# A new hand-written order of the engines' work in a fused HGRN2 and PReLU-network kernel

## The chip, the cores and the metric

The kernel runs on one core of one Trainium2 chip. The metric is the device time of one execution in microseconds (us). The kernel before took 596.71 us as the median of three runs (596.15, 596.71 and 600.7).

## The reference

Two blocks follow each other. The first is a gated linear attention (HGRN2) on q, k, v and f_logit of shape (4 batches, 8 heads, 768 tokens, 48); its output, bridged to 3072 tokens of 384, goes through a two-layer network with a PReLU.

```python
def _attn_ref(q, k, v, f_logit):
    f = 1.0 / (1.0 + np.exp(-f_logit))
    state = np.zeros((B, H, D, D), dtype=np.float32)
    for t in range(S):
        state = f[:, :, t, :, None] * state + np.einsum('bhd,bhe->bhde', k[:, :, t], v[:, :, t])
        y[:, :, t] = np.einsum('bhd,bhde->bhe', q[:, :, t], state)

def _moe_ref(x, w_in, w_out, alpha):      # w_in 384 x 2048, w_out 2048 x 384
    h = x @ w_in
    g = np.maximum(h, 0.0) + alpha * np.minimum(h, 0.0)
    return g @ w_out
```

## The kernel before, in words

The work is cut into 12 steps. Step n takes batches 2·(n % 2) and the one after it, and chunk n // 2 of 128 tokens (`steps`, L937). A step has an attention part, which gives xT (384 x 256 tokens), and a network part on that xT. The attention of step n+1 is laid between the network of step n, so that TensorE (PE) always has work.

Each step's work is split into some sixty closures, and `ORDER_WORDS` (L41 to L88) is a list of words, one for each closure; the loop at L957 calls them in that order. The scheduler is set to manual for PE, VectorE and ScalarE, so each engine's queue holds its instructions in just this order; the DMA issues of SP and POOL follow the same list. A word is the step's number and a key: `5r0` is the raw scores of step 5's first batch, `4Na3` the fourth slice of step 4's network. The keys that matter here:

- Loads. `e`: f, q, k and v of the step (L305 to L323), on POOL's queue except in step 0. Each load waits until the last reader of the tile before it is done.
- Gates and scans. `f` (ScalarE: the sigmoid at L329, then copies), `F` (VectorE lags at L338), `g` (ScalarE copies of the scores, L365), `G`, `h`, `i`, `k`, `l`, `p`, `q`, `t`: chiefly VectorE scans and products, some ScalarE copies.
- Scores. `r0`, `r1`: raw scores on PE (`scored`, L576; 64 loads and matmuls each); `R0`, `R1`: their copying to ad on VectorE (L599). `u0`, `u1`: scores by quads on PE (`scored4`, L585); `U0`, `U1`: their copying (L451). `o`: off-diagonal scores on PE (L566), `O`: copies on ScalarE (L573). `A0`, `A1`: placing in A on ScalarE (L606).
- State and output. `K`: the keys turned by way of DRAM, four DMA writes (`turned`, L473) and one read (`ksn`, L475), both on SP's queue. `d`: the state's increments on PE (L539); `D`, `M`: the state on VectorE (L544). `y0`, `y1`: the output products on PE (L614); `Y0`, `Y1`: their copies on ScalarE (L494). `X`: y to DRAM and back as xT (L503 to L505).
- Network, first layer. `Nx`, `Ny`, `Nz`: xh, xl and xs made from xT on ScalarE; `NY`, `NZ`: adding DMAs on POOL's queue (xl<-xT, xs<-xl, L823). `Na0` to `Na7`: the eight slices of x·w_in on PE (L831). From step 3, slices 3 to 6 go by parts: two passes in `Na`, a scaling on ScalarE in `Nq`, and a third pass with xs in `Nb`. `Nr` (ScalarE, L854) and `Nc` (VectorE, L859) apply the PReLU.
- Network, second layer. From step 1 its product is done in seven block products `Np0` to `Np6` (banks pa, pc, pb, pa, pd, pe, pf; L886), whose operands are sums of the gate made by `Nm`, `Nu`, `Nv`, `Nw` on VectorE (L880). `Nk`, `Ng` (ScalarE, L917 and L921) and `Nd`, `Ne`, `Nf`, `Nh`, `Ni`, `Nj`, `Nl`, `NL` (VectorE, L896) put the output together; `Ns0`, `Ns1` store it on SP's queue.

PSUM is held by two pools. `psa` has two pairs of banks, for raw, qu, off, pd, py and pk of the attention; `psn` has four banks for the network. A product that needs a bank waits until the bank's last reader is done.

```python
    with tc.manual_schedule(engines={mybir.EngineType.PE, mybir.EngineType.DVE, mybir.EngineType.Activation}):
...
        for key in ORDER:
            run[key]()
```

Of the kernel before, what the change touches and what calls it, by code (L numbers as in the profile page):

```python
# [40 lines left out]
ORDER_WORDS = """  # L41
0e 1e 0I0 0f 0F 0G 0g 0h 0i 0m 0p 0j 0r0 a0 0r1 0I1 0l 0I2 0R0 0I3 0I4 0I5 a1 0q 0o 0O 0k a2 0s 0t 0K0 w0 0u0 0U0
0R1 0J0 0H0 1f 0J1 0J2 0u1 0U1 0K1 0A0 1F w1 0d 0D 0J3 0H1 0J4 0A1 0J5 w2 0y0 0J6 0Y0 b0 0y1 0M 1G 0x0 0Y1 1r0 1g
1R0 0x1 0X a3 1h a4 0J7 1i w3 1r1 a5 2e 0Na0 0Nr0 0Na2 1R1 b1 w4 0Na1 0Na3 a6 1j 0Nc0 w5 0Nr1 v0 0Na4 0Na5 0Nc1 1m
0Nr2 1l 1k 0Nr3 a7 0Nc2 0Nr4 1o b2 v1 1K0 w6 b3 w7 0Nc3 0Na6 1K1 1p 0Nc4 1O 0Na7 v2 b4 1q 0Nr5 0Nc5 1u0 0Nr6 b5 0Nc6
0Nr7 v3 2f 1U0 0Nc7 b6 1u1 1U1 0Np0 1H0 1A0 2F 1H1 v4 1s 0Np1 0Np2 v5 1d b7 v6 V 1t v7 0Np3 0Np4 1D 1A1 1y0 1y1 2g
1Y0 0Np5 W0 1Y1 1X W1 W2 0Np6 W3 2G 1Na0 W4 W5 0Np7 0No0 1M 2h 0No1 2i Y3 1Na3 1Nr0 1Na1 Y4 Y5 2p 1Nr1 2q W6 Y6 1Na2
1Na4 1Nr2 2r0 2u0 2l W7 1Nc0 1Na5 1Nr3 1Nc1 2k 1Nm0 1Nr4 2K 1Nc2 2t 1Nc3 1Nm1 1Nc4 1Na6 1Nr5 2R0 1Nr6 2r1 2U0 2u1
1Nc6 2R1 1Na7 2A0 3e 1Nr7 1Nc5 2o 2U1 1Np0 Z3 2O 1Nc7 2d Z4 1Nk 1Np2 2D 2A1 3f 3F 1Np1 2y0 2y1 2Y0 1Np3 2Y1 2X 1Nu0
3g 1Nu1 1Nv0 3G 1Np4 1Nd 1Nv1 1Nw0 1Ng 1Nw1 1Ne 1Nj 1Nh 1Np5 3h 1Np6 1Nf 3p 1Nl 1Ni 3i 2Na2 2Na0 2M 1NL 2Na1 2Nr0 3l  # L50
3t 2Nr1 2Na3 3q 2Na4 2Nr2 3r0 3u0 2Nc0 2Nr3 3k 2Nc1 2Nm0 3K 2Nc2 3R0 3U0 2Nc3 2Na5 2Nm1 2Nr4 3r1 2Nr5 3o 3R1 2Na6
3A0 4e 2Nc5 3u1 2Nr6 2Nc4 3O 3U1 1Ns1 Z5 2Na7 2Nc6 Z6 3A1 3d 3D 1Ns0 2Np0 2Nr7 2Np1 2Nk 2Nc7 4f 2Nd 3y0 T 3y1 4F 3M
# [9 lines left out]
5Nz 5NZ 5Na5 6K 5Nc2 5Na4 6R0 5Nr7 5Na3 6U0 5Nc7 6r1 5Nq3 6A0 6u1 6R1 6U1 5Nq4 7e 5Nb3 5Nq5 4Ns0 5Na6 5Nb4 6o 5Nr3
5Nq6 5Nc3 6O 6A1 6d 5Nm1 5Nb6 5Nb5 6D 5Nr4 5Nr5 5Np0 5Nr6 5Nc4 5Nc6 7f 6y0 5Nc5 7F 6y1 5Nk 7g 6Y0 6Y1 5Np2 5Np1 6X
6M 5Np3 5Nu0 5Ng 5Nu1 5Nv0 5Nv1 5Nw1 7G 5Np4 6Nx 6Ny 5Nw0 5Nd 5Ne 7h 5Nj 5Nh 5Np5 5Np6 5Nf 7p 5Nl 5Ni 5Ns1 6Nz 6NY
6Na0 7i 7l 6Nr0 6Na1 5NL 6Na2 7k 7q 6Nr1 6Nc1 6Nr2 6Nc0 6Na7 6Na3 6Nm0 7r0 7K 6Nc2 7u0 7R0 6Nr7 6NZ 7t 7U0 7A0 6Na5
6Na4 6Nq4 7u1 6Nq3 6Nc7 7r1 6Nq5 6Na6 7R1 5Ns0 7U1 6Nq6 8e 6Nb3 6Nr3 6Nc3 6Nb4 6Nm1 6Nb6 6Nb5 7o 6Nr4 6Nr5 7A1 7O
# [5 lines left out]
9r0 9p 7Nl 7Ni 7Ns1 8Nz 8NY 8Na0 8Na7 9i 8Nr0 8Na1 7NL 8Na2 9k 8Na5 9l 9q 9u0 9t 8Nr1 8Nr2 8Nc0 8Na3 9R0 8Nc2 8Nc1
9K 8Nr7 8Na4 8NZ 8Nm0 9U0 8Nq4 9A0 8Nq3 8Nq5 9r1 9u1 8Na6 8Nc7 9R1 9U1 8Nq6 10e 8Nb3 8Nb4 8Nr3 8Nc3 8Nm1 8Nb6 8Nb5
8Nr5 9o 7Ns0 8Nr4 8Nc5 9A1 8Nr6 9O 9d 8Np0 8Nc4 9D 8Nk 8Np1 8Nc6 10f 9y0 9y1 8Np2 10F 9Y0 9Y1 10g 9X 9M 8Np3 8Nu0
8Nu1 10G 8Np4 9Nx 8Nd 10r0 8Nv0 8Nv1 8Nw0 8Ng 8Np5 8Ne 8Nw1 10h 9Ny 8Nh 8Nj 8Np6 8Nf 10p 8Nl 8Ni 9Nz 9NY 9Na0 9Nr0
8NL 10i 9Na1 9Na2 10k 10l 9Na7 10q 10t 9Nr1 9Nr2 9Nc0 9NZ 9Nc2 9Nc1 10K 9Nr7 10R0 8Ns1 9Na3 9Nm0 9Nc7 9Na4 10u0 10U0
9Na5 9Nq3 9Nq4 9Nb4 9Nq5 8Ns0 9Na6 10A0 9Nq6 11e 9Nb3 10r1 9Nr3 10u1 9Nb5 9Nc3 10R1 9Nb6 9Nm1 9Nr4 9Nr5 9Np0 10U1
9Nr6 9Nc6 10o 9Nc5 10d 10A1 10O 9Nc4 10D 11f 9Nk 9Np1 9Np2 10y0 10M 11F 9Nd 11G 10y1 10Y0 10Y1 9Np3 9Ng 11g 10X 9Nu1
9Nu0 9Nv0 9Np4 9Nv1 9Nw0 9Np5 9Ne 9Nw1 10Nx 9Nj 9Nh 11h 9Np6 9Nf 11p 9Nl 9Ni 10Ny 9NL 10Nz 10NY 10Na0 11i 9Ns1 10Nr0
10Na1 10Na2 10NZ 11k 11l 11q 10Na7 11r0 11t 10Nr1 10Nr2 10Nc0 10Nc2 11u0 10Nc1 10Nr7 10Nm0 11R0 11K 10Na3 11U0 10Nq3  # L80
10Na4 10Nq4 11A0 9Ns0 10Na6 10Nq6 10Nc7 10Na5 10Nb3 10Nb4 11u1 10Nr3 11r1 10Nr4 10Nc3 10Nq5 10Nm1 10Nb6 11R1 10Nb5
10Nr5 10Np0 11d 11U1 10Nr6 10Nc5 11o 10Nc6 11A1 10Nc4 11O 11D 10Nk 10Np1 10Np2 10Nd 10Nu0 11y0 10Nu1 11y1 11Y0 10Nv0
10Nv1 11Y1 11M 11X 10Np3 10Nw0 10Ng 10Ne 10Nw1 10Np4 10Np5 10Nj 11Nx 10Nh 11Ny 11Na7 10Nf 10Nl 10Ni 11Nz 11NY 11Na0
10Np6 11Nr0 11Na1 10NL 11Na2 11Nc0 11Na3 10Ns1 11Nr1 11Nc1 11Nm0 11Nr2 11Na4 11NZ 11Nc2 11Nr7 11Na5 11Nq3 11Nq4
10Ns0 11Na6 11Nq5 11Nb3 11Nc7 11Nq6 11Nb4 11Nr3 11Nb5 11Nc3 11Nr4 11Nr5 11Nm1 11Nb6 11Np0 11Nc4 11Nr6 11Nc5 11Nc6
11Nk 11Np1 11Np2 11Nd 11Np3 11Nu0 11Nu1 11Nv0 11Nv1 11Np4 11Nw0 11Ng 11Ne 11Nw1 11Np5 11Nj 11Nh 11Nl 11Np6 11Nf 11Ni
# [928 lines left out]
```

## Time and profile before

| | |
|---|---|
| median of three runs | 596.71 us (596.15 to 600.7) |
| profiled execution | 601.4 us, its span 599.6 us |
| PE busy, matmuls | 97% of the span, 8,200 |
| PEld busy (weight loads) | 89%, 8,200 |
| VectorE (DVE) busy | 84%, 1,027 instructions |
| ScalarE (ACT) busy | 50%, 561 instructions |
| GpSimd (POOL) busy | 11%, 114 instructions |
| mean granted TensorE clock | 0.982 |
| DMA | 67.57 MB, 113 GB/s in the mean |

All times within the profile count from the span's start. In a timeline row the first number is the start and the second the length in us; a number in brackets at the end is the idle time before the instruction and what released it ("issue": nothing that the profile shows), and x at the end a count of like instructions taken together. In the view of waits the three numbers are us in total, times, and the longest.

### The profile page before, as it was taken

How to read it: one execution, taken by the hardware profiler on the slowest of the kernel's cores; microseconds unless marked ns; L12 is line 12 of the kernel's file. 1: busy time of each engine (PE TensorE's matmuls, PEld its weight loads, DVE VectorE, ACT ScalarE, POOL GpSimd, SP SyncE). 2: the span in 40 equal slices, each digit the busy share in tenths (PEclk: the TensorE clock that was granted, in tenths of full speed). 3: DMA queues.
4: the chain of work that ended last, by engine and by line, in shares of the span. 5: the costliest groups of instructions: out<-in, count | busy, mean ns of one | idle time of the engine just before them, and what ended most of it. 6: DMA issues, size and time to landing. Idle time of an engine off the chain costs nothing.

```text
span 599.6 us, 18858 instructions
## 1 busy us (share of the span) xinstructions
PE 582.6 (97%) x8200; PEld 530.7 (89%) x8200; DVE 506.5 (84%) x1027; ACT 301.9 (50%) x561; POOL 68.5 (11%) x114
## 2 busy tenths in 40 slices
...
GB/s 300 348 159 375 62 54 28 178 54 54 177 56 93 190 56 79 184 52 91 173 72 67 137 109 80 151 107 80 140 119 80 125 133 52 109 47 29 80 1 26
DMA packets 69443, 67.57 MB, mean 113 GB/s; under 512 B 44689, under 2 KB 58641, under 8 KB 69361
## 3 DMA queue, kind: packets, MB, share of 16 engines
...
q8 instruction: 64, 1.05, 0.7%
...
q14 instruction: 19, 0.15, 0.1%
...
## 4 chain that ended last, share of the span: by engine, by line
PE 83%; DVE 8%; ACT 6%; issue 2%; DMA 1%; ACTq 0%; DVEq 0%
PE ph L831 39%; PE pa L886 7%; PE pe L886 5%; PE pf L886 5%; PE pd L886 4%; PE qu L591 4%; PE pc L886 3%; PE pb L886 3%; PE raw L582 3%; PE po L866 3%; PE py L614 3%; DVE qd L338 2%; ACT A L606 2%; PE pd L539 1%; DVE ad L451 1%
## 5 line engine op out<-in xcount | busy, mean ns | idle before, releaser
L831 PE MATMUL ph<-xT,w_in_sb 128*128 128x256 f32 x612 | 136.9, 380 | 0.4 <-DMA xT<-y 0.3
L831 PEld LDWEIGHTS ph<-xT,w_in_sb 128*128 128x128 f32 x612 | 115.1, 190 | 16.8 <-issue 0.9
L854 ACT ACTIVATE gate<-ph 128x512 f32<-128x512 f32 x96 | 55.0, 595 | 121.2 <-PE ph L831 107.6
L859 DVE SCALAR_TENSOR_TENSOR gate<-gate,om,ph 128x256 f32<-128x256 f32 x192 | 81.2, 475 | 31.3 <-ACT gate L854 31.0
L886 PE MATMUL pa<-w_out_sb,gate 128*128 128x192 f32 x352 | 61.7, 329 | 0.0
L880 DVE TENSOR_TENSOR gate<-gate 128x512 f32<-128x512 f32 x88 | 57.5, 687 | 3.6 <-PE pb L886 2.8
L886 PEld LDWEIGHTS pa<-w_out_sb,gate 128*128 128x128 f32 x352 | 57.1, 190 | 0.5
L451 DVE COPY_PREDICATED ad<-mquad,qu 128x224 f32<-128x224 int32 (+6 forms) x140 | 42.2, 301 | 6.8 <-PE qu L591 1.6
L599 DVE COPY_PREDICATED ad<-mraw,raw 128x256 f32<-128x256 int32 (+1 forms) x96 | 42.6, 444 | 5.9 <-PE raw L582 3.3
L606 ACT COPY A<-ad 32x256 f32<-32x256 f32 x96 | 38.7, 403 | 11.7 <-DVE ad L451 10.2
L844 ACT ACTIVATE ph<-ph 128x512 f32<-128x512 f32 x36 | 20.0, 570 | 37.6 <-PE ph L831 25.1
L440 DVE TENSOR_TENSOR scores<-scores,fs 128x768 f32<-128x768 f32 (+5 forms) x60 | 37.4, 623 | 1.6
L831 PE MATMUL ph<-xh,hi 128*128 128x256 f32 x216 | 35.3, 300 | 0.0
L831 PE MATMUL ph<-xl,lo 128*128 128x256 f32 x216 | 32.7, 289 | 2.2 <-issue 2.2
L424 ACT COPY A<-q 48x512 f32<-48x512 f32 x44 | 27.1, 617 | 15.2 <-DVE q L398 14.8
L886 PE MATMUL pb<-t,gate 128*128 128x192 f32 x176 | 31.5, 331 | 0.5 <-DVE gate L859 0.5
L886 PE MATMUL pd<-t,gate 128*128 128x192 f32 x176 | 30.6, 327 | 1.0 <-DVE gate L880 1.0
L831 PEld LDWEIGHTS ph<-xh,hi 128*128 128x128 f32 x216 | 29.4, 194 | 2.5 <-issue 1.2
L831 PEld LDWEIGHTS ph<-xl,lo 128*128 128x128 f32 x216 | 29.3, 197 | 2.4 <-issue 2.4
L338 DVE TENSOR_TENSOR qd<-qd,f 128x768 f32<-128x768 f32 (+2 forms) x36 | 27.2, 754 | 4.6 <-ACT qd L331 4.6
L886 PE MATMUL pe<-w_out_sb,gate 128*128 128x192 f32 x176 | 30.6, 327 | 0.4 <-DVE o L896 0.4
L323 POOL DMA_DIRECT2D vs<-in_v x22 | 13.2, 605 | 154.6 <-PE py L614 154.4
...
## 6 DMA issues: line engine op xcount, KB each, us to landing
...
```

Source lines behind the costliest of these rows:

```text
L338: nc.vector.tensor_tensor(qdv[d], qdv[d - 1][:, :, :, 1:5 - d], f[:, :, 1:5 - d].rearrange("p (g i) r -> p g i r", i=NB), ALU.mult)
L424: nc.scalar.copy(A[halves(cc)[1], :, par * HP:(par + 1) * HP, CH * cc:CH * (cc + 1)], x["q3"][rows(par)].rearrange("p (u h c) s t -> p u h ...
L440: nc.vector.tensor_tensor(by_four(us[:, :, UO[m]:UO[m] + 4 * n]), by_four(us[:, :, skip:skip + 4 * n]), spread(fq[:, :, 1:1 + n], n), ALU. ...
L451: nc.vector.copy_predicated(ad[:, u, :, :, 4 * m:DB], mquad[:, lo:lo + n].bitcast(I32).unsqueeze(1).unsqueeze(1).broadcast_to((128, 2, HP, ...
L591: nc.tensor.matmul(qu[DB * j:DB * (j + 1), par, hp * QS + 4:hp * QS + QL], lhsT=x["k4"][r_, g * DB:(g + 1) * DB], rhs=x["us"][r_, g, 4:QL] ...
L599: nc.vector.copy_predicated(adu[:, :, :, d:4], mraw[:, d, :, d:4].bitcast(I32).unsqueeze(1).broadcast_to((128, H, NB, n)), rv[:, :, QO[d]: ...
L606: nc.scalar.copy(A[s_, u, :, s_], ad[s_, u].rearrange("p r h t -> p (r h) t"))
L831: nc.tensor.matmul(banks[f][:, j * T:(j + 1) * T], lhsT=of[:, kt, 128 * j:128 * (j + 1)], rhs=by[:, kt], start=first_ and kt + j == 0, sto ...
L854: nc.scalar.activation(to, of, AF.Relu, scale=-1.0)
L859: nc.vector.scalar_tensor_tensor(to[:, j], to[:, j], om[:, m:m + 1], of[:, j], ALU.mult, ALU.add)
L880: nc.vector.tensor_tensor(block(to)[:, p], block(x_)[:, p], block(y_)[:, p], op)
L886: nc.tensor.matmul(banks[to][:, 0:DH], lhsT=block(of)[:, f], rhs=of_w_out(by)[:, f], start=start and f == 0, stop=f == NH - 1, skip_group_ ...
```

## The change: the same words in another order

Only `ORDER_WORDS` is changed. It holds the same words as before, each once; no closure, tile, pool or queue differs, and every engine gets the same number of instructions of each kind (PE 8,200 matmuls). On PE at least 36 of 331 words stand elsewhere, on VectorE 42 of 470, on ScalarE 33 of 312, on SP 13 of 61, on POOL 2 of 29.

The main moves:

- PE: `4r0` from behind the first products of network 3 to between `2Np3` and `2Np4`. `5r0` from beside `5u0` to ahead of `4Na0`, so that five slices of network 4 lie between the two. `8r0` and `8u0`, which stood together, have `7Na3` and `7Na7` between them, and `7Na4` goes behind `8u0`. `10r0` between `8Np3` and `8Np4`, `9r0` one word earlier. Two slices of network 2 between `3u0` and `3r1`, and `3o` behind `2Na7 2Na6`. In steps 6 and 7 almost nothing moves (`6Na4` and `6Na5` change places).
- ScalarE: xs earlier (`3Nz`, `4Nz`, `5Nz` ahead of `Nr0` of their step, where they stood behind it). `7g` behind `6Y0 6Y1`. `8f` ahead of `7O`. `9g` behind `8Y0 8Y1`.
- VectorE: `6M` behind `5Nd` and `7G` earlier; `8U0` ahead of `7Nc7`; `8q` behind `7Nc0`; `9R0` ahead of `9i`; `2M` ahead of `1Nw1`.
- SP: stores (`Ns0`, `Ns1`) behind the turned keys or the tokens of the next step. POOL: the loads of step 3 go q, f, k instead of q, k, f; network 5's xs<-xl goes ahead of the load of q for step 7, which it followed.

The stretch from `2Np2` on, which shows the moves of `4r0`, `3Nz` and the first part of step 4:

```diff
-3Y0 3Y1 2Np2 2Np3 2Nu1 2Nu0 4G 2Np4 3X 2Nv0 4g 2Nv1 2Nw0 2Ng 3Nx 3Ny 2Nw1 2Ne 2Nj 2Nh 2Np5 4h 2Np6 2Nf 4p 2Nl 2Ni
-3Na0 4i 3Nr0 2NL 3Na2 3NY 4k 4l 4q 2Ns1 3Nz 3Na1 4t 3Nr1 3Na7 3Na4 3Nr2 3Nc0 4K 3Nc2 3Nc1 4r0 3Nr7 3Nm0 4u0 3Nc7
-3Na6 3NZ 2Ns0 4R0 3Na3 4U0 4r1 3Na5 4u1 3Nq3 3Nq4 4A0 3Nq5 4R1 4U1 3Nq6 4o 4O 5e 3Nb3 3Nr3 3Nc3 3Nb4 3Nm1 3Nb6 3Nb5
+2Np2 1Ns0 3Y1 3M 4g 2Np3 4r0 2Nu1 2Nu0 2Np4 3X 2Nv0 4G 2Nv1 2Nw0 2Ng 3Nx 3Ny 2Nw1 2Ne 2Nj 2Nh 2Np5 4h 2Np6 2Nf 2Nl
+4p 3Na1 3Nz 3Na0 4i 3Nr0 2NL 2Ni 4k 4l 3NY 3Na2 4q 3Nr1 3Na7 4K 3Na3 5e 2Ns1 3Nr2 3Nc0 3NZ 3Na4 3Nc2 4t 3Nc1 3Nr7
+3Nm0 4u0 3Nc7 4R0 4U0 3Nq3 3Na6 4r1 4A0 4R1 3Na5 4u1 4U1 3Nq4 3Nq5 3Nq6 4o 4O 3Nb3 3Nr3 3Nc3 3Nb4 3Nm1 2Ns0 3Nb6
```

Step 5 between the products of network 4:

```diff
-3Nw0 3Ng 5G 3Np4 4Nx 4Ny 3Nw1 3Nd 3Ne 5h 3Nj 3Nh 3Np5 3Np6 3Nf 5p 3Nl 3Ni 4Na0 5i 4Nr0 3NL 4Na2 4NY 5k 4Na5 5l 3Ns1
-4Nz 4Nq5 4Na1 5q 5t 4Nr1 4Nc0 4Nr2 5r0 5u0 4Nc1 4Nm0 5K 4Nc2 5R0 4NZ 4Na3 5U0 4Na7 4Nr7 4Na4 5r1 5A0 4Nq3 4Nq4 5u1
-4Nc7 5R1 5U1 4Na6 4Nb4 6e 4Nb3 5o 4Nq6 4Nr3 5d 5O 4Nc3 5A1 4Nm1 5D 4Nb6 4Nb5 4Nr4 4Nr5 4Np0 4Nr6 5y0 3Ns0 4Nc4 4Nc5
+5G 3Nv1 3Nw0 3Ng 3Np4 4Nx 4Ny 3Nw1 3Nd 3Ne 5h 3Nj 3Np5 3Np6 3Nh 3Nf 3Nl 5p 3Ni 5r0 4Nz 4Na0 5i 4Nr0 4Na1 3NL 5k 4NY
+4Na5 5l 4Nq5 4Na2 5q 4Nr1 5K 4Na3 4Nc0 4Nr2 5u0 5t 4Nc1 4Nm0 4Nc2 5R0 5U0 4Na7 4Nr7 4NZ 4Na4 6e 3Ns1 5r1 4Nc7 4Nq4
+4Nq3 5A0 5u1 5R1 5U1 4Na6 4Nb5 4Nb3 5o 4Nq6 4Nr3 5d 5O 4Nc3 4Nb4 5A1 4Nm1 5D 4Nr4 4Nr5 4Nb6 4Np0 4Nr6 5y0 4Nc4 4Nc5
```

Step 7 and 8, at the words that moved:

```diff
-5Nr6 5Nc4 5Nc6 7f 6y0 5Nc5 7F 6y1 5Nk 7g 6Y0 6Y1 5Np2 5Np1 6X
+5Nr6 5Nc4 5Nc6 7f 6y0 5Nc5 5Nk 7F 6y1 6Y0 5Np2 6Y1 5Np1 6X 7g
...
-6Nc4 6Nr6 7d 6Np0 8f 6Nc5 7D 6Nk 6Np1 7y0 8F 7y1 6Nc6 7Y0 7Y1 7X 6Np2 8g 7Nx 7M 6Np3 6Nu0 6Nu1 8G 6Np4 6Nv0 6Nd 6Nv1
+6Nr6 7d 8f 6Np0 7O 6Nc5 7D 6Nk 6Np1 7y0 8F 7y1 6Nc6 7Y0 6Np2 7Y1 7X 8g 7Nx 7M 6Np3 6Nu0 6Nu1 6Np4 6Nv0 6Nd 6Nv1 6Nw0
...
-8t 8r0 7Nr2 7Nc0 7Nc1 8u0 8R0 7Nm0 7Na7 8K 7Nc2 7Nr7 7Na3 7Nc7 7NZ 7Na5 8U0 7Nq3 7Nq4 8r1 8u1 7Nq5 8A0 6Ns0 7Na6 8R1
+7Nr2 7Nc0 8q 7Nc1 8R0 9e 6Ns1 8K 7Na3 7Nm0 7Na7 8u0 7Nc2 7Nr7 7NZ 7Na4 8U0 7Na5 7Nq3 7Nq4 8r1 8u1 7Nq5 8A0 7Na6
```

More of the change, by code (lines that the diff above doesn't have):

```diff
@@ L41 @@
 ORDER_WORDS = """
[L42 to L51, printed above, removed]
@@ L52 @@
-3A0 4e 2Nc5 3u1 2Nr6 2Nc4 3O 3U1 1Ns1 Z5 2Na7 2Nc6 Z6 3A1 3d 3D 1Ns0 2Np0 2Nr7 2Np1 2Nk 2Nc7 4f 2Nd 3y0 T 3y1 4F 3M
-3Y0 3Y1 2Np2 2Np3 2Nu1 2Nu0 4G 2Np4 3X 2Nv0 4g 2Nv1 2Nw0 2Ng 3Nx 3Ny 2Nw1 2Ne 2Nj 2Nh 2Np5 4h 2Np6 2Nf 4p 2Nl 2Ni
-3Na0 4i 3Nr0 2NL 3Na2 3NY 4k 4l 4q 2Ns1 3Nz 3Na1 4t 3Nr1 3Na7 3Na4 3Nr2 3Nc0 4K 3Nc2 3Nc1 4r0 3Nr7 3Nm0 4u0 3Nc7
-3Na6 3NZ 2Ns0 4R0 3Na3 4U0 4r1 3Na5 4u1 3Nq3 3Nq4 4A0 3Nq5 4R1 4U1 3Nq6 4o 4O 5e 3Nb3 3Nr3 3Nc3 3Nb4 3Nm1 3Nb6 3Nb5
-4d 3Nr4 3Nr5 3Np0 4D 4A1 3Nr6 3Nc6 3Nc5 4y0 3Nc4 4y1 5f 4M 4Y0 4Y1 3Np2 3Np1 3Nk 5F 4X 3Np3 3Nu0 5g 3Nu1 3Nv0 3Nv1
@@ L62 @@
[L62 to L66, printed above, removed]
@@ L72 @@
[L72 to L76, printed above, removed]
@@ L77 @@
[L77 to L86, printed above, removed]
@@ L87 @@
-11NL 11Ns1 11Ns0
+0e 1e 0I0 0f 0F 0G 0g 0r1 0h 0i 0m 0p 0j 0r0 0I1 0l 0I2 a0 0R0 0I3 0I4 0I5 0q 0o a1 0k a2 0O 0s 0t w0 0u0 0U0 0R1
+0K0 0H0 1f 0J0 0J1 0J2 w1 0K1 0u1 0J3 0U1 1F 0A0 0d 0D 0H1 0A1 w2 1G 0J4 0J5 0y0 0Y0 b0 0J6 0y1 0x0 0Y1 0M 1g 1i 0J7
+1r0 0x1 1R0 0X a3 1h a4 b1 w3 a5 1m 1r1 w4 1j 0Na0 v0 0Nr0 0Na1 0Na2 1R1 0Na3 a6 0Nc0 w5 0Nr1 0Na4 0Na5 0Nc1 2e 0Nr2
+1l 1k 0Nr3 a7 0Nc2 1o b2 0Nr4 1K0 1p 1O v1 w6 w7 0Na7 1K1 0Nc3 0Nc4 b3 v2 b4 0Na6 1q 0Nr5 0Nc5 1u0 0Nr6 b5 0Nc6 0Nr7
+v3 1u1 1s 2f 1U0 0Nc7 b6 1U1 1H0 1A0 2F 1t 0Np0 v4 0Np1 0Np2 v5 1d b7 v6 V 1H1 1D v7 2g 0Np3 0Np4 1A1 1y0 1y1 1Y0
@@ new lines @@
+0Np5 W0 1Y1 1X W1 Y3 W2 0Np6 W3 2G 1Na0 W4 W5 0Np7 0No0 2h 1M 0No1 2i 1Nr0 1Na1 Y4 Y5 1Na3 2p 1Nr1 2q W6 1Na2 1Na4
+Y6 3e 1Nr2 2u0 2l 1Nc0 1Nr3 2t 1Nc1 2k 1Nm0 1Nr4 1Nc2 2r0 1Nc3 W7 1Nm1 1Na5 1Nc4 1Na6 1Nr5 2R0 1Nr6 2r1 2U0 2K Z3
+2u1 1Nc6 2R1 2A0 1Na7 1Nr7 1Nc5 2o 1Np0 2U1 2O 3f 1Nc7 2d Z4 1Nk 2D 2A1 1Np2 3F 1Np1 2y0 2y1 1Np3 2Y0 2Y1 2X 1Nu0
+1Nu1 1Nv0 3G 3g 1Np4 1Nd 1Nv1 1Nw0 1Ng 2M 1Nw1 1Ne 1Nj 1Nh 1Np5 3h 1Np6 1Nf 1Nl 3p 1Ni 3i 1NL 2Na0 3l 4e 2Nr0 2Na1
+2Nr1 2Na3 2Na2 1Ns1 3q 2Nr2 3r0 3u0 2Nc0 2Nr3 3k 3t 2Nc1 2Nm0 3R0 3U0 2Na5 2Nc2 2Nc3 2Nm1 2Na4 Z5 2Nr4 3r1 2Nr5 3K
```

34 lines of the change are left out of this document (29 added, 5 removed).

## The prediction, made before the change was run

> **What bounds the kernel now.** I read the page first: busy shares, the share of the chain, and the DMA queues.
>
> ```profile
> PE 582.6 (97%) x8200; PEld 530.7 (89%) x8200; DVE 506.5 (84%) x1027; ACT 301.9 (50%) x561; POOL 68.5 (11%) x114
> ...
> q8 instruction: 64, 1.05, 0.7%
> ...
> PE 83%; DVE 8%; ACT 6%; issue 2%; DMA 1%; ACTq 0%; DVEq 0%
> ```
>
> TensorE carries the chain and has no spare share; the change leaves all its matmuls in place. So a new order can only win back the microseconds in which PE stands. I therefore went to the view of waits for PE and PEld, which names what ended each stand:
>
> ```profile
> PE pd L886 <- DVE gate L880: 1.0, 2, 0.7
> PE pb L886 <- DVE gate L859: 0.5, 1, 0.5
> PE pe L886 <- DVE o L896: 0.4, 1, 0.4
> PE qu L591 <- DVE ad L451: 0.2, 1, 0.2
> ...
> PEld ph L831 <- issue: 5.2, 16, 2.4
> ...
> PEld qu L591 <- issue: 3.0, 5, 1.7
> ...
> PEld off L566 <- issue: 2.0, 5, 1.1
> ```
>
> Two kinds are seen: PE waits for VectorE (five stands, 2.1 us), and PE stands on "issue", in which no engine is late. The largest of the second kind, in the timeline of PEld (start, us, idle before):
>
> ```profile
> 204.60 0.73 PEld L582 LDWEIGHTS raw<-qd,k 48*32 48x32 f32 x64
> ...
> 206.15 0.79 PEld L831 LDWEIGHTS ph<-xl,lo 128*128 128x128 f32 x6
> 207.08 0.83 PEld L591 LDWEIGHTS qu<-scores,k 48*32 48x32 f32 x64
> ...
> 209.13 0.58 PEld L566 LDWEIGHTS off<-q,kh 48*32 48x32 f32 x57 [1.08 <-issue]
> 209.75 2.33 PEld L831 LDWEIGHTS ph<-xs,sum 128*128 128x128 f32 x19
> ```
> ```profile
> 253.68 0.36 PEld L591 LDWEIGHTS qu<-scores,k 48*32 48x32 f32 x28 [1.67 <-issue]
> 254.22 1.35 PEld L831 LDWEIGHTS ph<-xh,hi 128*128 128x128 f32 x6 [0.17 <-issue]
> 255.45 1.40 PEld L831 LDWEIGHTS ph<-xl,lo 128*128 128x128 f32 x6
> ```
> ```profile
> 349.35 1.02 PEld L831 LDWEIGHTS ph<-xl,lo 128*128 128x128 f32 x6 [2.40 <-issue]
> 350.25 2.89 PEld L831 LDWEIGHTS ph<-xs,sum 128*128 128x128 f32 x13
> ```
>
> They break off in the middle of a word (7 of 64 loads of 4o, 36 of 64 of 5u1, within 6Na6), so they are no wait of the program. What are they? The windows between them, with PE, PEld, DVE, ACT and POOL busy (count), granted clock, DMA share and GB/s:
>
> ```profile
> 208.80:253.50 44.70, 43.12 (x634) 40.53 (x633) 40.86 (x86) 22.41 (x42) 5.22 (x7) 1.00 0.43 105
> 253.50:349.20 95.70, 93.09 (x1394) 87.59 (x1394) 85.39 (x178) 46.21 (x87) 10.44 (x14) 0.98 0.44 108
> ```
> ```profile
> 251.40:254.30 2.90, 1.47 (x95) 1.06 (x79) 2.24 (x6) 2.39 (x6) 0.72 (x1) 0.98 0.85 223
> 346.10:349.40 3.30, 1.11 (x19) 0.82 (x7) 2.87 (x7) 2.05 (x5) 0.72 (x1) 1.00 0.88 295
> 240.00:260.00 20.00, 18.57 (x446) 16.77 (x448) 14.77 (x42) 8.80 (x18) 2.20 (x3) 0.91 0.65 154
> ```
>
> Queue q8 moves 1.05 MB in 64 packets; PE has 16,400 matmuls and loads, so a packet is 256 of them. Between the first two stands lie 1,267 recorded instructions, between the last two 2,788: five and eleven times 256 (1,280 and 2,816), 1% short of it as some records are missing. So PE stands where the next 256 instructions have not come, and it does while the DMA engines are 0.85 to 0.88 busy. In the 20 us around the second stand the granted clock means 0.91.
>
> [...]
>
> What fills the DMA engines there? The SP and POOL timelines of step 5's loads (DMA issue; the idle before it):
>
> ```profile
> 238.61 0.87 POOL L823 DMA_DIRECT2D xs<-xl  x1 [7.73 <-ACT xs L820]
> 241.25 0.74 POOL L313 DMA_DIRECT2D q<-in_qT  x1 [1.77 <-DVE f L418]
> 249.26 0.74 POOL L313 DMA_DIRECT2D f<-in_fT  x1 [7.27 <-DMA turned<-f]
> ```
> ```profile
> 239.06 6.15 SPq L473 DMA_DIRECT2D turned<-f  x4
> 248.69 0.33 SPq L475 DMA_DIRECT2D ksn<-turned  x1
> ```
> ```profile
> 382.73 3.25 SPq L473 DMA_DIRECT2D turned<-f  x4
> 390.42 0.33 SPq L475 DMA_DIRECT2D ksn<-turned  x1
> ```
>
> In step 5 the network's xs (4NZ) and q go out together with the four turned writes; ksn follows 9.6 us behind them and f at once behind it, 2 us ahead of the stand. In step 8, with no xs beside them, ksn follows after 7.7 us.
>
> **The change, part by part.** Counts are equal on every engine (PE 8,200 matmuls; POOL and SP the same DMAs), so nothing is added or removed, and the cost of the moved instructions themselves is zero: PE runs back to back and each takes its time wherever it stands. What differs are the stands.
>
> (a) 4r0 moves between 2Np3 and 2Np4. 2Np4 (pd) now waits for 2Nu on VectorE: it is the longer one of the two pd waits, 0.7 us.
>
> 4r0's 64 loads take 0.73 us (row at 204.60) and lie in that gap: −0.6. If 4F is late, 4r0 itself waits and the term is 0. What follows 4r0's old place moves up.
>
> (b) 5Np5 waits 0.4 us for 5Nd (the pe wait); 6M now stands behind 5Nd on VectorE: −0.4 (0 if 7G, which is earlier on VectorE now, is late behind 7g).
>
> (c) 6Np2 waits 0.5 us for 6Nc6 (the pb wait), which stands behind 8F, which needs 8f. On ScalarE 8f stood behind 7O:
>
> ```profile
> 357.07 1.27 ACT L573 COPY A<-off 32x256 f32<-32x256 f32 x4
> ...
> 358.99 1.06 ACT L329 ACTIVATE f<-f 128x1024 f32<-128x1024 f32 x1
> ```
>
> Now 8f goes ahead of 7O; 1.27 us is more than 0.5, but something of VectorE's own length may be late next: −0.3. The 0.2 us of 8u1 behind 8U0 goes with 8U0 ahead of 7Nc7: −0.2. These four make −1.5, between −1.8 (all rows) and 0.
>
> (d) The stand in 4o, 1.08 us. 3Nz on ScalarE goes ahead of 3Nr0, so POOL's xs<-xl is issued earlier and the turned writes, ksn and f of step 4 run with less beside them and end ahead of PE's block. −0.9, between −1.08 and +1 (the stand doubled).
>
> (e) The stand in 5u1, 1.67 us, and the slow loads behind it: 1.35 + 1.40 against twice 0.79 (row at 206.15) is 1.2 us. 4Nz goes ahead of 4Nr0, from behind it:
>
> ```profile
> 236.98 0.60 ACT L854 ACTIVATE gate<-ph 128x512 f32<-128x512 f32 x1 [7.35 <-PE ph L831]
> ```
>
> It waited only for the order, since 4Nr0 waits 7.35 us for PE, and xs<-xl 7.73 for it; xs is issued up to 7 us earlier and is through before the turned writes. These should then take 7.7 us instead of 9.6, ksn and f come 1.9 us earlier, and the block finds free engines. Against it: 5r0 now stands ahead of 4Na0 and 4Na3 ahead of 5u0, so the stretch ahead of the stand gets shorter. Over the last 300 instructions (a length I assume for PE's look ahead) it loses 12 loads of 4Na3 by 0.13 us (0.79/6) for 12 of 5u0 by 0.013 (0.83/64): 1.4 us less time for the block to come. So the gain of 1.9 us is nearly spent. Bounds −2.9 and +1.9 (a stand as long as the longest, 2.40, and its clock tail); I take −2.0, nearer to the gain, because the burst then starts ahead of the packet and not with it.
>
> (f) The stand in 6Na6, 2.40 us, with the slow loads behind it: 13 at 0.22 (2.89/13) against 0.12 (2.33/19), 1.3 us. PE's order there stays. 6Y0 and 6Y1 go ahead of 7g on ScalarE:
>
> ```profile
> 311.88 0.67 ACT L365 COPY scores<-qd 128x256 f32<-128x256 f32 x1
> ...
> 315.99 1.07 ACT L494 COPY y<-py 128x512 f32<-128x512 f32 x2
> ```
>
> y stood behind 7g's copies, of which this is the first; the tokens, xT, xl and xs come up to 4 us earlier, and the store of step 4 goes behind the four turned writes. So the burst runs earlier against an unchanged PE. 7G gets its scores about 1 us later and has no taker on PE before 7r0. Bounds −3.7 and 0; I take −2.2.
>
> (g) New costs. 8u0 and 8u1: 7Na7 and 7Na3 now stand ahead of 8u0, so the last 300 instructions before a block due in 8u1 lose 12 whole loads of L831 by 190 ns for loads of 13 ns: 2.1 us less, in a step whose ksn and f burst lies there too. Nothing stands there now; bounds 0 and 2.4 plus 1.3, I take +0.5. 4Na3 follows 4Na0, 4Na1, 4Na5 and 4Na2 directly, takes the bank that 4Nc0 frees, and may wait for one gated half (475 ns): 0 to 0.5, +0.2.
>
> ```profile
> L831 PEld LDWEIGHTS ph<-xT,w_in_sb 128*128 128x128 f32 x612 | 115.1, 190 | 16.8 <-issue 0.9
> ...
> L859 DVE SCALAR_TENSOR_TENSOR gate<-gate,om,ph 128x256 f32<-128x256 f32 x192 | 81.2, 475 | 31.3 <-ACT gate L854 31.0
> ```
>
> The opening, steps 9 to 11, and the stores that go later on SP: 0; PE does not stand there, and a store's only taker is the reuse of o two steps on.
>
> Sum: −1.5 −0.9 −2.0 −2.2 +0.5 +0.2 = −5.9 us on the profiled execution's 601.4 (span 599.6), so 595.5. That execution is 4.7 us above the median of 596.71 and near the slowest of the three, 600.7. If the median run has all these stands, it comes to 590.8; if it lacks the slow clock (2.5 us, 1.7 of them in the sum), to 592.5. I take 592.0.
>
> **The rivals.**
> R1, the holds don't move: their places are counts of PE instructions, which the change leaves as they are, and the median run, 4.7 us shorter than the profiled one, may not have the three stands at all. Then only the VectorE waits go: 596.7 − 1.5 = 595.2. For it: the 4.7 us. Against it: the DMA share of 0.85 and more in each stand. [...]
>
> R2, slower: the shorter stretches of (e) and (g) decide. If the block of 256 takes longer than PE's stretch ahead of 5u1 and of 8u1, both stand as long as the longest now does, 2.40 us and a clock tail of 1.3. Against the present 2.9 at 5u1 that is +0.8, at 8u1 +3.7; with the stand in 6Na6 kept and 4o's and the VectorE waits gone (−1.1 −1.5), +1.9: 598.6, and 600 if the median run now lacks the tail at 5u1. It decides from about 1.5 us of delay in ksn and f.
>
> R3, larger: all stands of (d), (e), (f) go with their tails, no new one comes: 1.1 + 2.9 + 3.7 + 1.5 = 9.2, 596.7 − 9.2 = 587.5.
>
> **How the numbers follow.** Forecast (590 to 594.5) 0.42, R1 (594.5 to 598) 0.23, R3 (587 to 590) 0.20, R2 (above 598) 0.15. The range 587.0 to 598.0 leaves out R2 and little of R3. About 1% is what a measurement of this kernel tells from no change: 590.7 and 602.7. Below 590.7 lie R3 and 0.15 of the forecast: 0.35. Above 602.7 half of R2, with whatever I did not see in it: 0.07. Between: 0.58.
>
> **What would show it.** In the new profile: no DVE gate wait ahead of pd at 2Np4, and 4r0 there; xs<-xl issued before its step's turned writes; ksn within 8 us of them in steps 5 and 7; PEld "issue" under 0.5 us in 4o, 5u1 and 6Na6; clock 1.00 at 250 and 350 us. Wrong: stands of over 1 us at the same counts, a new one in 8u1, or PE waits for VectorE that were not there.

## The result, and the profile after

The changed kernel takes 595.5 us (median of 20 runs, 593.45 to 601.11); the kernel before, run beside it, 597.94 (20 runs, 596.15 to 600.7). The ratio is 0.9961, 95% interval 0.9943 to 0.9979. Timed again (12 runs) it was 0.9948 (0.9929 to 0.9966). So the change is a gain of 0.4 to 0.5%, about half of the 0.8% forecast (592.0 from 596.71), and its size is what has to be explained. The profiled execution of the changed kernel took 593.86 us, span 592.1; that of before 601.4, span 599.6. Between these two lie 7.5 us, three times the difference of the medians.

The page of the changed kernel, the lines that answer to those of before:

```profile
span 592.1 us, 18853 instructions
...
PE 580.1 (98%) x8200; PEld 527.9 (89%) x8200; DVE 505.7 (85%) x1027; ACT 300.4 (51%) x561; POOL 68.4 (12%) x114
...
q8 instruction: 64, 1.05, 0.7%
```

Its view of waits:

```profile
PE pd L886 <- DVE gate L880: 0.3, 1, 0.3
...
PEld ph L831 <- issue: 3.4, 15, 0.6
...
PEld off L566 <- issue: 1.9, 5, 0.8
PEld qu L591 <- issue: 1.7, 5, 0.4
```

All the waits for VectorE that the prediction listed are gone (the pd wait of 0.3 us was there before too, as the second of the two). The longest stand on "issue" in ph fell from 2.4 to 0.6 us, in qu from 1.7 to 0.4. In off it fell only from 1.1 to 0.8. Its timelines of PEld, at 4o and at 6Na6:

```profile
208.66 0.58 PEld L566 LDWEIGHTS off<-q,kh 48*32 48x32 f32 x57 [0.81 <-issue]
```
```profile
343.70 0.66 PEld L831 LDWEIGHTS ph<-xl,lo 128*128 128x128 f32 x5 [0.55 <-issue]
```

4o again breaks off after 7 of 64 loads. In 5u1 there is no break: its 64 loads stand in one row (251.38, 0.85 us).

One reading of the prediction can be made exact here. The 1,267 and 2,788 instructions between the stands of before are short of 1,280 and 2,816 not because records are missing: PE's queue also holds 13 and 28 semaphore instructions there, which the views leave out. With them the distances are five and eleven times 256 to the instruction. And f of step 5 went out 2.75 us ahead of the stand (253.68 − 1.67 − 249.26), not 2.

### The profile page after: what moved, and what is told of

Its sections match the earlier page's. It is cut to its first block, busy times and chain, and to the rows that moved or that the text cites. A ratio compares the mean times of both kernels' runs of the same rounds, so it can differ in the third digit from the quotient of the medians.

```text
span 592.1 us, 18853 instructions
## 1 busy us (share of the span) xinstructions
PE 580.1 (98%) x8200; PEld 527.9 (89%) x8200; DVE 505.7 (85%) x1027; ACT 300.4 (51%) x561; POOL 68.4 (12%) x114
## 3 DMA queue, kind: packets, MB, share of 16 engines
q8 instruction: 64, 1.05, 0.7%
## 4 chain that ended last, share of the span: by engine, by line
PE 80%; issue 10%; DMA 4%; ACT 3%; DVE 3%; POOL 1%; POOLq 0%; ACTq 0%; DVEq 0%
PE ph L831 36%; PE pa L886 9%; PE pd L886 5%; PE pf L886 5%; PE pe L886 5%; PE pb L886 5%; PE pc L886 4%; PE py L614 3%; PE qu L591 3%; PE raw L582 3%; DMA w_out_raw<-in_w_out 2%; PE pd L539 1%; PE off L566 1%; DVE ad L451 1%; DMA f<-in_fT 1%
## 5 line engine op out<-in xcount | busy, mean ns | idle before, releaser
L599 DVE COPY_PREDICATED ad<-mraw,raw 128x256 f32<-128x256 int32 (+1 forms) x96 | 42.7, 445 | 8.9 <-PE raw L582 6.2
L886 PE MATMUL pc<-t,gate 128*128 128x192 f32 x176 | 30.6, 327 | 0.0
L886 PE MATMUL pf<-w_out_sb,gate 128*128 128x192 f32 x176 | 30.5, 327 | 0.0
```

Of the source, the lines that this page charges most:

```text
L599: nc.vector.copy_predicated(adu[:, :, :, d:4], mraw[:, d, :, d:4].bitcast(I32).unsqueeze(1).broadcast_to((128, H, NB, n)), rv[:, :, QO[d]: ...
L886: nc.tensor.matmul(banks[to][:, 0:DH], lhsT=block(of)[:, f], rhs=of_w_out(by)[:, f], start=start and f == 0, stop=f == NH - 1, skip_group_ ...
```

## The experiments

**Are the stands the same in every execution?** The kernel before and the changed one were profiled again, unchanged, to see how far one profile stands for the median.

> The kernel before, unchanged, for a second profile. Theory T1 (the stands of PE on its instructions come and go from execution to execution, and the first profiled execution, 601.4 us, was an unlucky draw): a time of 597 to 599 us and smaller stands: the sum of the stands in 4o, 5u1 with its slow loads, and 6Na6 with its slow loads is under 4 us, against 7.7 us in the first profile. Theory T2 (the stands are fixed by the order): the same three stands within 0.5 us each, and a span within 2 us of 599.6.

> The kernel before, unchanged, for a third profile. Theory: the three stands with their slow loads (4o, 5u1, 6Na6) make 7.7 us in the first profile (601.4 us) and 6 us in the second (599.3 us); in an execution near the median of 597.5 they make about 4 us, so the sum follows the time one for one. Rival: they make 6 us and more in an execution near the median too, and the spread of the times lies elsewhere.

> The kernel before, unchanged, for a fourth profile; the same theory and rival as for the third: the sum of the three stands with their slow loads follows the execution's time one for one, at about 4 us for 597.5, or it does not.

> The changed kernel, unchanged, for a second profile. T1: a time of 595 to 597 us, and a stand of over 1 us on PE's instructions somewhere that the first profile of it (593.86 us, stands of 0.9 in 4o and 0.6 in 6Na6) does not show. T2: 593 to 594.5 us and the same two stands.

The profiled executions took 599.26, 598.23 and 597.89 us (before) and 595.54 us (changed). The rows of the stands in 5u1 and 6Na6 in the second profile of before:

```profile
253.70 0.36 PEld L591 LDWEIGHTS qu<-scores,k 48*32 48x32 f32 x28 [1.94 <-issue]
...
348.74 0.77 PEld L831 LDWEIGHTS ph<-xl,lo 128*128 128x128 f32 x6 [1.70 <-issue]
```

and in the third:

```profile
254.21 0.36 PEld L591 LDWEIGHTS qu<-scores,k 48*32 48x32 f32 x28 [0.57 <-issue]
...
347.69 0.78 PEld L831 LDWEIGHTS ph<-xl,lo 128*128 128x128 f32 x6 [0.82 <-issue]
```

The places are fixed to the load (28 of 64 to go in 5u1 each time), the lengths are not. I added up, for each profile, by how much the words around 4o, 5u1 and 6Na6 exceed the lower quartile of like words in the first profile, slow loads included:

| execution | time, us | excess at the three places, us |
|---|---|---|
| before, first | 601.4 | 8.3 |
| before, second | 599.26 | 6.7 |
| before, third | 598.23 | 5.8 |
| before, fourth | 597.89 | 4.7 |
| changed, first | 593.86 | 1.5 |
| changed, second (with 8u1) | 595.54 | 3.2 |
| changed, third (with 8u1) | 595.58 | 3.6 |

From the first to the fourth the time falls by 3.5 us and the excess by 3.6: in these four profiles the spread of the times is for the most part these stands, and the profile on which the sum was made had almost twice as much of them as the fourth, the one nearest to the median. Other boundaries have stands as well: the third profile has one of 0.73 us in 5d and slow loads behind 4o (24 in 4.43 us instead of 2.92). So the second profile of before fits neither theory that was written down for it (its 6Na6 fell from 2.40 to 1.70 us, but its three places did not fall under 4), the third and fourth follow the theory that time and excess go together, and the second of the changed kernel is the first theory's: 595.54 us, with 1.66 us in 6Na6. The last row is from the second timing of the changed kernel:

> The changed kernel, unchanged, timed on the same chip beside the one above. If the medians add up from the parts (0.9964 and 0.9983 for the two parts, 0.9 us lost in the opening, 0.3 us at 8u1): 0.996 to 0.997 of before. Rival (its first profile, 7.5 us under that of before, is what it is worth): 0.990 or below.

It took 595.35 us in the median of 12 runs, before 598.27: 0.9948, a little more gain than the 0.996 to 0.997 expected; of these, 0.996 lies within the interval. The rival, 0.990, does not.

**The parts by themselves.** Two kernels took over one kind of move each.

The first (e1) puts 6M behind 5Nd, 8f ahead of 7O, 8U0 ahead of 7Nc7, and

```diff
-3Y0 3Y1 2Np2 2Np3 2Nu1 2Nu0 4G 2Np4 3X 2Nv0 4g 2Nv1
+3Y0 3Y1 4g 2Np2 2Np3 4r0 2Nu1 2Nu0 4G 2Np4 3X 2Nv0 2Nv1
```

The second (e2) puts 3Nz, 4Nz and 5Nz ahead of 3Na0, 4Na0 and 5Na0, and

```diff
-7F 6y1 5Nk 7g 6Y0 6Y1 5Np2 5Np1 6X
+7F 6y1 5Nk 6Y0 6Y1 5Np2 5Np1 6X 7g
```

> The kernel before with only the moves that answer PE's waits for VectorE: 4r0 (with 4g) between 2Np3 and 2Np4, 6M behind 5Nd, 8f ahead of 7O, 8U0 ahead of 7Nc7. T1: the waits of 0.7, 0.4, 0.5 and 0.2 us go, in the median as in the profile, so 1.2 to 1.8 us faster than before. Rival (the waits are filled from other stands, and PE stands for its instructions instead): less than 0.6 us faster.

> The kernel before with only the moves that send the network's inputs earlier: 3Nz, 4Nz and 5Nz ahead of the first product of their network, and 7g behind 6Y0, 6Y1 and 6X. T1: it works on stands that not every execution has, so 0.5 to 1.5 us faster in the median, and 4 us and more against the first profile. Rival T2: the three stands are there in each execution and go: 3 us and more faster in the median. Rival T3 (earlier transfers change nothing at these stands): within 0.4 us of before.

e1: 595.88 us against 597.27, ratio 0.9983 (0.9967 to 0.9998), and its view of waits has only the 0.3 us of pd. The prediction's −1.5 for these terms stood: −1.4, with an interval from −0.1 to −2.0 us, so the size is not sharply known. e2: 594.72 us, 0.9964 (0.9946 to 0.9982), −2.6 us. That lies between the first theory's 0.5 to 1.5 and the second's 3 and more, and the interval (−1.1 to −3.2 us) excludes neither; the third, no change, is out. In e2 PE's order is that of before, word for word; four words moved on ScalarE, and with them the transfers that follow them. Its rows at 4o, 5u1 and 6Na6:

```profile
207.42 0.75 PEld L566 LDWEIGHTS off<-q,kh 48*32 48x32 f32 x64
...
250.15 0.85 PEld L591 LDWEIGHTS qu<-scores,k 48*32 48x32 f32 x64
...
343.37 0.76 PEld L831 LDWEIGHTS ph<-xl,lo 128*128 128x128 f32 x6 [0.89 <-issue]
```

Two of the three stands are gone in that execution, with nothing changed in PE's order.

> The kernel before with the moves of the two partial kernels together (for VectorE's waits: 4g, 4r0, 6M, 8f, 8U0; for the early inputs: 3Nz, 4Nz, 5Nz, 7g). The opening and steps 8 to 11 stay as before. Theory that both gains stand on their own: 1.4 + 2.5 = 3.9 us faster than before (0.9935), and so faster than the whole change by 1 us and more. Rival (what one part wins the other loses, as PE only meets its next stand sooner): 2 to 2.8 us, as the whole change.

Together: 593.25 us (8 runs), 0.994 (0.9906 to 0.9974), −4.4 us. By this figure the two gains add up; the rival's 2 to 2.8 us is less, but lies within the interval (−1.6 to −5.6 us), so it is not excluded. This kernel has only nine of the moved words.

**What the whole change loses again: the opening.** All three profiles of the changed kernel start 1Na0 at 90.9 to 91.1 us, those of before at 89.7 to 90.2. PE from 28 us on, before and changed:

```profile
29.29 1.53 PE L539 MATMUL pd<-vs,ksn 64*48 64x48 f32 x64
30.75 2.33 PE L935 MATMUL off_0a<-ones 128*128 128x256 f32 x6
```
```profile
29.22 1.22 PE L935 MATMUL off_0a<-ones 128*128 128x256 f32 x2
30.37 1.53 PE L539 MATMUL pd<-vs,ksn 64*48 64x48 f32 x64
```

The idle matmul 0J3 (out off_0a, from ones) goes ahead of 0d and takes 1.2 us, in which 0d could have run. ScalarE shows who is late for it:

```profile
31.97 0.96 ACT L556 COPY vs<-pd 48x384 f32<-48x384 f32 x2 [0.76 <-PE pd L539]
```

```diff
- 0u1 0J3 0U1 1F 0A0 0d 0D
+ 0u1 0U1 1F 0A0 0d 0D 0J3
```

> The changed kernel with one word put back: the idle matmul 0J3 behind 0d and 0D, as before, where the change has it ahead of 0d. Theory: this one idle matmul holds 0d, the copy of vs behind it, and so 0y0 and all that follows; 1Na0 starts at 89.9 us, about 1.1 us earlier than in the two profiles of the changed kernel (90.9 and 91.1), and the kernel is about 1.0 us faster than it: 0.994 to 0.995 of before. Rival (the opening's loss has several causes): 1Na0 starts at 90.5 or later.

With 0J3 back, 0Na0 starts at 41.8 us instead of 42.7 to 42.9, as in before (41.8 to 42.0), and 1Na0 at 90.3: 0.9 and 0.6 to 0.8 us earlier. The 1Na0 expected was 89.9, the rival's 90.5 or more, so it is most of the loss and not all. The time is 594.97 us, 0.9949 (0.9924 to 0.9973); against the changed kernel's own 0.9961 and 0.9948 that alone would show nothing.

The third profile of the changed kernel does not follow this account. There 0J3 took only 0.70 us and 0y0 started at 33.36 us, within the 33.20 to 33.44 of before; but 0y0 then took 1.83 us instead of 1.15, at a granted clock of 0.50 between 34 and 36 us (1.00 in the first profile), and 0Na0 came at 42.86 all the same. So the order holds 0d up in two of the three profiles; what the clock does there e3 does not test.

**Is it the fetching of instructions?** Kernel e5 shifts every later PE instruction by 56 places, in the same order.

```diff
-        for _ in range(IDLE):
-            idled(idle, 0)
+        for _ in range(2 * IDLE):
+            nc.tensor.matmul(idle[:, 0:128], lhsT=ones[:, 0:128], rhs=ones[:, 0:128], start=True, stop=True)
```

> The kernel before with the 14 idle matmuls ahead of all work split into 28 of half the width, so that PE's work is the same but every later instruction stands 56 places later in its queue. Theory that PE stands where a block of 256 instructions has not come: the stands come 56 instructions earlier in the work, so not in 4o but in 4u1 ahead of it with about 22 of its 64 loads to go, in 5u1 with about 56 of 64 to go instead of 28, and not in 6Na6 but in 7r1 with about 22 of 64 to go. Rival (the stands belong to the words): in the same words at the same loads.

```profile
214.24 0.24 PEld L591 LDWEIGHTS qu<-scores,k 48*32 48x32 f32 x19 [1.67 <-issue]
...
310.72 0.12 PEld L539 LDWEIGHTS pd<-vs,ksn 64*48 64x48 f32 x1 [1.63 <-issue]
...
353.55 0.28 PEld L582 LDWEIGHTS raw<-qd,k 48*32 48x32 f32 x21 [1.16 <-issue]
```

The stands moved off 4o and 6Na6 into 4u1 and 7r1, with 21 of 64 loads to go (the first row has 19, two more lie in a later row), where 22 were expected. 5u1 shows none this time, where a full 56 to go were expected; 6d, which had none, has one, and there are others (2.18 us in 0d, 0.88 us in a slice at 447.66). The one execution took 606.64 us; its opening was longer too (0d 3.0 us over its usual length instead of 0.6 to 1.2, 0Na0 1.9 us over). Places are counts of instructions: that shows, from one execution, what the prediction only argued.

**Is it the load on the DMA engines?** Kernel e6 adds 512 KB to each step's burst.

```diff
-            nc.sync.dma_start(out=ksn.rearrange("p u n -> p (u n)"), in_=way)
+            spare = dram.tile([128, W], F32, tag="spare", name=f"spare_{i}", bufs=2); nc.sync.dma_start(out=spare, in_=way); nc.sync.dma_start(out=ksn.rearrange("p u n -> p (u n)"), in_=way)
```

> The kernel before with one transfer more in every step from step 2 on: the turned keys, 512 KB, are also copied to a spare place in DRAM, just ahead of ksn; nobody waits for the copy. Theory that the blocks of instructions are late because the DMA engines are full there: the stands in 4o, 5u1 and 6Na6 grow by 1 us and more each or new ones of that size come at other blocks, and the kernel is 4 us and more slower. Rival (a block takes its time whatever else moves): within 0.6 us of before.

605.82 us, 1.0132 (1.0084 to 1.018). Longer stands on "issue" came in 2o and 5d, at other boundaries (2o is new; 5d has one of 0.7 to 1.2 us in three other profiles too, the third of before among them):

```profile
120.11 0.21 PEld L566 LDWEIGHTS off<-q,kh 48*32 48x32 f32 x15 [1.88 <-issue]
```
```profile
262.48 1.21 PEld L539 LDWEIGHTS pd<-vs,ksn 64*48 64x48 f32 x54 [2.29 <-issue]
```

but the three old ones did not grow (1.08, 0.31 and 1.98 us), and 1.7 us of the loss is a plain wait of 3d for the delayed ksn:

```profile
169.43 0.94 PE L539 MATMUL pd<-vs,ksn 64*48 64x48 f32 x64 [1.72 <-DMA ksn<-turned]
```

So it speaks for the theory, and not cleanly: the load of the DMA engines matters, but the run does not show that it acts on the block alone.

**Which transfer holds the block in 4o and 6Na6?** In the changed kernel the turned writes of step 7 run in 6.6 us instead of 9.6 before (SP, then POOL):

```profile
330.59 3.94 SPq L473 DMA_DIRECT2D turned<-f  x4
337.19 0.33 SPq L475 DMA_DIRECT2D ksn<-turned  x1
```
```profile
337.74 0.74 POOL L313 DMA_DIRECT2D f<-in_fT  x1 [7.42 <-DVE ad L599]
```

yet the second and third profile have stands of 1.66 and 1.94 us in 6Na6:

```profile
344.94 0.66 PEld L831 LDWEIGHTS ph<-xl,lo 128*128 128x128 f32 x5 [1.66 <-issue]
```
```profile
345.18 0.66 PEld L831 LDWEIGHTS ph<-xl,lo 128*128 128x128 f32 x5 [1.94 <-issue]
```

The load of f for step 8 goes out at 337.74 us, 5.4 us ahead of the stand (343.70 − 0.55); before, as the next rows show, it went out at 344.44, 2.5 us ahead of it (349.35 − 2.40). It landed 5.1 us later in the changed kernel, at 342.84, and 5.7 us later in before: so it fills the last microseconds ahead of the stand in the one and all of the stand in the other. In both f follows ksn by 0.55 us, since the turned writes read f's tile.

```profile
334.27 5.57 SPq L473 DMA_DIRECT2D turned<-f  x4
343.89 0.33 SPq L475 DMA_DIRECT2D ksn<-turned  x1
```
```profile
344.44 0.76 POOL L313 DMA_DIRECT2D f<-in_fT  x1 [10.23 <-DVE ad L451]
...
346.56 0.72 POOL L313 DMA_DIRECT2D k<-in_kT  x1 [1.36 <-PE raw L582]
```

Kernels e10 and e11 move this load, and that of f for step 5, behind the stands, with the words 5e and 8e behind 3Nb4 and 6Nb5, and put these two loads on ScalarE's queue instead of POOL's. All other transfers keep their queues; q, k and v, which the two words also carry, keep about their times (q to k 10.2 and 13.0 us, as in the changed kernel).

```diff
-            loads.dma_start(out=t.rearrange("p (u x) -> p u x", u=U),
+            (nc.scalar if name == "f" and (bp, c) in ((1, 2), (0, 4)) else loads).dma_start(out=t.rearrange("p (u x) -> p u x", u=U),
```

> The changed kernel with two loads moved: f of step 5 and f of step 8 go out from ScalarE's queue behind 3Nb4 and 6Nb5, after the stands in 4o and 6Na6, instead of from POOL's queue ahead of them. Nothing waits for them before 5f and 8f, some 6 to 9 us later. Theory that this load (512 KB) is what holds the block of instructions there: the stands (0.7 to 0.9 and 0.6 to 1.9 us in three profiles) fall below 0.3 us each, and the kernel is 1 to 2.5 us faster than the changed one: 0.991 to 0.993 of before. Rival (the turned writes, ksn and the loads of q and k hold it): stands of the same size, 0.995 of before. Rival (the load only holds the next block): a new stand of 0.5 us and more within 10 us behind them.

> The kernel with the two partial changes (593.25 us, 0.994 of before) and the same two loads of f moved to ScalarE's queue behind 3Nb4 and 6Nb5. The same theory: the stands in 4o and 6Na6 (0.95 and 0.64 us in its profile) fall below 0.3 us each, 0.990 to 0.9925 of before. Rivals as above: 0.994, with the same stands or with new ones behind.

e10, at 4o, at 6Na6 (its two passes), and the load of f, now on ScalarE's queue:

```profile
206.57 0.75 PEld L566 LDWEIGHTS off<-q,kh 48*32 48x32 f32 x64
```
```profile
340.51 0.77 PEld L831 LDWEIGHTS ph<-xh,hi 128*128 128x128 f32 x6
341.21 0.79 PEld L831 LDWEIGHTS ph<-xl,lo 128*128 128x128 f32 x6
```
```profile
343.08 0.38 ACTq L313 DMA_DIRECT2D f<-in_fT  x1
```

Both are gone, none of 0.5 us came behind them, and the time is 592.62 us, 0.9919 (0.9891 to 0.9946). e11: 592.6 us, 0.992 (0.9889 to 0.9951); no stand in 4o, 0.42 us left in 6Na6 where less than 0.3 was expected, and 0.62 and 0.69 us in 5u1 and 5d. So f's load held the blocks, whether by its time or by its queue, which these runs do not separate. These two have the lowest medians of this study. By the ratios e10 is 1.7 to 2.5 us under the changed kernel (0.9919 against 0.9961 and 0.9948), but the intervals overlap.

**Is it the block itself that comes late?** The traces hold every packet of q8. The block for 6Na6 in the first profile of before, seen between 346.9 and 347.0 us:

```profile
q8 instruction: 1, 0.02, 60.1%
```

The share is of 16 engines in that 0.1 us, so this packet took 0.96 us. The same for the other places; "entry" is the time at which PE entered the 256 instructions ahead of the boundary:

| execution, place | packet starts, us | behind the entry, us | PE goes on, behind the packet's end, us | stand, us |
|---|---|---|---|---|
| before, first, 4o | 206.76 | 2.0 | 1.4 | 1.08 |
| before, first, 5u1 | 251.45 | 5.1 | 1.3 | 1.67 |
| before, first, 6Na6 | 346.93 | 2.4 | 1.5 | 2.40 |
| changed, first, 5u1 | 247.05 | 0.8 | | none |
| changed, first, 6Na6 | 341.32 | 0.7 | 1.4 | 0.55 |
| e10, 4o | 204.14 | 0.7 | | none |
| e10, 6Na6 | 339.02 | 0.2 | | none |

In quiet places the packet starts some 0.8 us behind the entry, in the median, and takes 1.05 us. So a late block is not a slow packet but one that starts late, 2 to 5 us behind the entry in before. And the 256 instructions ahead of 6Na6 pass in 2.4 us only, most of them small scores: 0.7 + 0.95 + 1.4 us is already 0.6 us more, so there even a packet that starts as early as in quiet places leaves a stand. That is the changed kernel's first profile (0.55 us); its second and third have packets 1.7 and 2.2 us behind the entry, and stands of 1.66 and 1.94 us.

What the packet met on its way differs too. In the view of windows the numbers are the stretch, its length, busy us and count of PE, PEld, DVE, ACT and POOL, granted clock, DMA share and GB/s; the microsecond in which the packet starts in the changed kernel, and that in which it is under way in e10:

```profile
341.00:342.00 1.00, 1.00 (x105) 1.00 (x93) 0.86 (x3) 0.96 (x3) 0.00 (x0) 1.00 0.67 262
```
```profile
339.00:340.00 1.00, 1.00 (x98) 1.00 (x86) 0.97 (x4) 0.97 (x2) 0.00 (x0) 1.00 0.06 16
```

In e10 the block has the DMA engines to itself, a share of 0.06 and 16 GB/s, which is its own 16 KB.

Another remedy gives the block more time instead: slow products ahead of it, in the kernel e4.

```diff
-3Nq6 4o 4O 5e 3Nb3
+3Nq6 3Nb3 4o 4O 5e
...
-6Nc7 7r1 6Nq5 6Na6 7R1 5Ns0 7U1 6Nq6 8e 6Nb3
+6Nc7 6Na6 6Nb3 7r1 6Nq5 7U1 7R1 5Ns0 6Nq6 8e
```

> The two parts together as in the earlier kernel (593.25 us there, 0.994 of before), and two moves of products on PE more, at the two stands that are left: 3Nb3 goes ahead of 4o, and 6Na6 and 6Nb3 go ahead of 7r1 (with 7U1 ahead of 7R1 on VectorE). The places of the blocks, counted in instructions, stay; but the last 300 instructions ahead of the block that is late now hold more slow products and fewer fast score matmuls: about 0.6 us more time ahead of the one in 4o, 1.4 us more ahead of the one in 6Na6. Theory: those stands, 0.95 and 0.64 us in the earlier profile, fall below 0.4 us each, and the kernel is 0.5 to 1.5 us faster than that one, 0.990 to 0.993 of before. Rival (the delay only goes on to the next block, or VectorE waits for r1): 0.994 or slower.

593.98 us, 0.9941 (0.992 to 0.9963): no faster than e4, where 0.5 to 1.5 us less was expected. The stand in 4o is gone from its profile, and 0.57 us stay ahead of 6Na6 where less than 0.4 was expected; with this spread of times a gain of half a microsecond can't be told from none.

## Why the prediction was off

- *The base.* The sum was −5.9 us on an execution of 601.4, and the median was taken to lack only 1.7 us of it (the slow clock). That step failed first. The two executions of before nearest to the median have 4.7 and 5.8 us at the three places, not 8.3. The base also moved: 597.94 over 20 runs instead of 596.71 over three.
- *(a) to (c), VectorE's waits, −1.5.* Right: −1.4 alone in e1 (interval −0.1 to −2.0), and all four are gone.
- *(d), 4o, −0.9.* Too much. It is 0.70 to 0.89 us in the changed kernel's three profiles, 1.08 to 1.63 in the four of before: about −0.6. The step that failed is that the burst would run shorter and end ahead of the block. It went from 9.2 us (turned at 193.16, ksn at 202.39) only to 8.9 (193.21 and 202.13), though xs went out 1.7 us earlier, and f's load stayed on the block, before and changed:

```profile
202.93 0.75 POOL L313 DMA_DIRECT2D f<-in_fT  x1 [6.83 <-DMA turned<-f]
```
```profile
202.65 0.75 POOL L313 DMA_DIRECT2D f<-in_fT  x1 [6.50 <-DMA turned<-f]
```

- *(e), 5u1, −2.0.* Right in place, sign and mechanism: gone in all three profiles, the slow loads too. The burst ran in 8.1 us instead of 9.6, where 7.7 was forecast, and f came 2.0 us earlier (1.9 forecast):

```profile
238.60 3.18 SPq L473 DMA_DIRECT2D turned<-f  x4
246.69 0.33 SPq L475 DMA_DIRECT2D ksn<-turned  x1
```

In before the stand is 0.57 to 1.94 us, so worth less than the first profile said. The 1.4 us of shorter stretch, set against it, cost nothing seen; it was counted, like the 2.1 us in (g), over 300 instructions, a length that I assumed and that no run shows: the packets listed in the experiments start 0.2 to 5.1 us behind the entry into the 256 ahead of their boundary.
- *(f), 6Na6, −2.2.* Wrong: 0.55, 1.66 and 1.94 us after, 0.82 to 2.40 before. I counted that the transfers run earlier, and not that POOL then sends f earlier as well; the turned writes, which read its tile, held it back, and they end earlier too.
- *(g), 8u1, +0.5.* Near: 0, 0.55 and 0.42 us. The +0.2 for 4Na3's wait for a bank did not come.

The third profile of the changed kernel, at 8u1:

```profile
389.38 0.56 PEld L591 LDWEIGHTS qu<-scores,k 48*32 48x32 f32 x38 [0.42 <-issue]
```

- *The opening, 0.* Wrong: some +0.8 us at 0Na0 and +1.1 at 1Na0 in the mean of three profiles, e3 explaining most of it. "PE does not stand there" was true of PE's time and false of its order: the opening is a chain 0d, copy of vs, 0y0, and an idle matmul ahead of 0d is work on that chain. That is shown for two of the three profiles; in the third the slow 0y0 at a granted clock of 0.50 stands in its place.

In the sum, near the median: three places 4.7 to about 3.4 (with 8u1), VectorE's waits −1.4, opening +0.9 makes −1.8; with the third profile's 5.8 for before it makes −2.9. Measured are −2.4 and −2.9, so nothing is left that needs another cause, and no more can be told from so few profiles. R1 was nearest in its number (595.2), but that is luck: by its reason the stands would not be in the median, and they are. Of R2's longer stands in 5u1 and of R3's 587.5 nothing came.
